# Twelve units of attention loads, each in tiles of its own, and the order of the loads, keys and first weight rounding around them

## The chip, the cores and the metric

The kernel runs on one core of a Trainium2 chip. The metric is the device time of one execution in microseconds (us), lower is better. The core has five engines with an instruction stream each: TensorE (PE, matrix products), VectorE (DVE), ScalarE (ACT), GpSimd (POOL) and SyncE (SP, here only a queue that issues DMA transfers). Each engine takes its instructions strictly in the program's order and waits at the first one whose inputs aren't there.

## What is computed

A decaying linear attention (retention) over 2 batches, 8 heads, 768 positions and 64 channels, and behind it two feed-forward blocks without routing:

```python
for t in range(S):
    state = gamma[None, :, None, None] * state + np.einsum('bhd,bhe->bhde', k[:, :, t], v[:, :, t])
    y[:, :, t] = scale * np.einsum('bhd,bhde->bhe', q[:, :, t], state)
x = y.transpose(0, 2, 1, 3).reshape(B * S, H * D)      # 1536 tokens x 512
x = (x @ w_a) * (x @ w_b) @ w_out                      # hidden 1536
h = x @ w_in; y = np.maximum(0.01 * h, h) @ w_out2     # hidden 2048
```

All arrays are float32.

## The kernel before, in words

**Units.** Attention is cut into twelve units, 3 tiles of 512 tokens times 4 pairs of heads, tile by tile. A unit reads four arrays of 128 x 512 float32 (256 KB each): `qT`, `kT` (turned), `kn` and `vn` (plain); its tiles are called q, k, n and v. The first four units ("wide", u < NPAIR = 4) work in chunks of 128 positions, the other eight in chunks of 64. A unit goes through these steps, each a helper:

- keys (`wide_keys`, L519, `scaled_keys`, L583): kd, the keys n times a decay, on ACT. The wide form reads the constants `table`; the other reads `small`, a part of the tile `second`. Both tables are loaded by DMA (L915, L929)
- queries (`wide_queries`, L525, `scaled_queries`, L588): qs, the queries times a decay, on DVE for u < 2, else on POOL; the second form reads `second`
- scores (L532; L644 for the later units) on PE from k and qs, then P, the masked scores, on DVE (L538; `masked`, L650)
- states (L548; L644) on PE from v and kd, with a chain of small adds on DVE (cb, L552, L556; later units cr, L606, L608). For wide units `wide_spreads` (L562, ACT) copies cb into the tile wk
- within (L570; L644), P times v, and across (L577; L644), qs times the states (wk in the wide units), into one PSUM bank x
- `leave_x`: x is split on ACT and DVE into a rounded part and a remainder (x..h L248, x..l L249), and copied once more for two of the three tiles (xf, L659, L661, ACT). x00 to x03 are the first tile's four pairs, x20 to x23 the second's, x10 to x13 the third's

Every product of the feed-forward blocks is made of three passes of such splits (`mm3`, L254 to L256).

**The loop** runs u from -1 to 11. Turn u makes scores and states of unit u + 1 and within, across and `leave_x` of unit u; keys and queries are made two units ahead: unit 0's before the loop, unit 1's in the turn -1, unit u + 2's late in turn u, for u >= 0. The loads are three units ahead: `loads(u)` issues n, v, q, k of unit u on SP's queue into one of NLOAD = 3 sets of landing tiles, so a load has to wait until the unit three before it has read that set. Units 0 to 2 are loaded ahead of the loop.

**Weights between.** Raw weights (512 KB tiles `raw_a`, `raw_b`, L284) come through the same SP queue, at most NRAW = 4 ahead of the rounding. Each is rounded in three steps on ACT (`begin_weights`, L305, L307, L309) and three on DVE (`round_steps`, L323, L325, L327); then `high(key)` (ACT, L934) and `low()` (DVE, L940) split it into, say, a0h and a0l. `ROUND` says in which turn the steps on DVE run (a0 in 2, b0 in 4, a1 in 5, b1 in 6); `begin_weights` is issued at the end of the turn before, `high` at the end of the same turn, `low` in the next turn.

**Dense work.** `FILL` says how many steps of the first feed-forward products (pa and pb, twelve matmuls of 512 columns for one weight tile, three to a step) PE takes at the end of a turn: 3 in turn 3, 1 in turn 4, then 4 in each turn.

**Slots.** Nearly all big tiles come from one pool of NSLOT = 83 tiles of 256 KB; `slots.done(n)` only counts how many are free for what is planned later.

The order inside a turn of the wide units, before:

```python
if u >= 0:
    loads(u + NLOAD)
leave_x(u)
if u < NPAIR - 1:
    wide_spreads(u + 1)
...
for _ in turn:
    pass
if u >= 0:
    keys(u + 2)
    queries(u + 2)
```

Of the kernel before, what the change touches and what calls it, by code (L numbers as in the profile page):

```python
# [9 lines left out]
F32 = mybir.dt.float32  # L10
# [16 lines left out]
NPAIR = H // 2  # L27
# [8 lines left out]
NRAW = 4  # L36
NEXTRA = 10
NWARM = 10
FILL = {3: 3, 4: 1, 5: 4, 6: 4, 7: 4, 8: 4, 9: 4, 10: 4, 11: 4}
PUMP = {7: 1.2, 8: 1.6, 9: 0.6, 10: 0.6, 11: 0.6}  # L40
ROUND = {2: ("a", 0), 4: ("b", 0), 5: ("a", 1), 6: ("b", 1)}
NBLOCK = 2
NLOAD = 3
CPT = TT // P
COUNT = {"a": FF1, "b": FF1, "wo": FF1, "wi": FF2, "wq": FF2}
HALF = FF2 // 2
# [180 lines left out]
def retention_moe_kernel(ctx: ExitStack, tc: tile.TileContext, ins, out):  # L227
    nc = tc.nc
    qT, kT, kn, vn, wab, wo, w2, head, grow, fine = ins
# [7 lines left out]
    slots = Slots(main, NSLOT)  # L237
# [7 lines left out]
    def split(src, name, new=slots.new):  # L245

        hi, lo = new(F32R, name + "h"), new(F32R, name + "l")
        nc.scalar.copy(hi, src)  # L248
        nc.vector.tensor_sub(lo, src, as32(hi))  # L249
        return hi, lo  # L250
# [24 lines left out]
    source = {"a": (wab, 0), "b": (wab, 1), "wo": (wo, 0), "wi": (w2, 0), "wq": (w2, 1)}  # L275
# [3 lines left out]
    def load_weights():  # L279
        if at["load"] < len(order) and at["load"] < at["round"] + NRAW:  # L280
            kind, f = order[at["load"]]
            src, i = source[kind]
            t = rawp.tile([P, TT], I64, tag="raw", name=f"raw_{kind}{f}")
            nc.sync.dma_start(t, src[f, i])  # L284
            raws[kind, f] = t
            at["load"] += 1
# [7 lines left out]
    def begin_weights():  # L294
        for _ in begin_steps():
            pass
# [16 lines left out]
    def round_steps():  # L313


        n = at["round"]
        key = order[n]
        if key not in begun:
            begin_weights()
        u, sl = begun.pop(key)  # L320
        raws.pop(key)
        ui = u.bitcast(I32)
        nc.vector.tensor_scalar(u, u, TOP, None, op0=ALU.min)  # L323
        yield
        nc.vector.tensor_scalar(ui, ui, 3, None, op0=ALU.logical_shift_left)  # L325
        yield
        nc.vector.tensor_tensor(ui, ui, sl, op=ALU.add)  # L327
        rounded[key] = u
        at["round"] += 1
        load_weights()  # L330
        if key in parked:
            dram[key] = park.tile([P, TT], F32, tag=f"{key[0]}{key[1]}", name=f"{key[0]}{key[1]}")
            nc.gpsimd.dma_start(dram[key], rounded.pop(key))
            slots.done(1)
# [147 lines left out]
    for w in spread:  # L482
        nc.gpsimd.memset(w[0:D, :, 0:D], 0.0)
        nc.gpsimd.memset(w[D:P, :, D:P], 0.0)
    units = [(n, p) for n in range(NTILE) for p in range(NPAIR)]
    landing = {
        name: [slots.new(F32, f"{name}{i}") for i in range(NLOAD)] for name in ("n", "v", "q", "k")
    }
    un = {}
    x, xf = {}, {}  # L490
    heads = [slice(h * D, (h + 1) * D) for h in range(2)]
# [8 lines left out]
    def loads(u):  # L500
        if u >= len(units):
            return
        d = un[u] = {}
        for name, src in (("n", kn), ("v", vn), ("q", qT), ("k", kT)):
            d[name] = landing[name][u % NLOAD]
            nc.sync.dma_start(d[name], src[units[u]])

    flip = heads[::-1]
    cols = [slice(j * P, (j + 1) * P) for j in range(CPT)]
# [17 lines left out]
    @known  # L527
    def wide_scores(u, t, p, d):
        sc = [bank(f"sc{u}{h}") for h in range(2)]
        for c in cols:  # L530
            for h, r in enumerate(flip):
                nc.tensor.matmul(sc[h][:, c], d["k"][r, c], d["qs"][r, c], start=True, stop=True)  # L532
        d["P"] = []
        m = causal.rearrange("p (o t) -> p o t", o=1).to_broadcast([P, CPT, P])
        for h in range(2):
            d["P"].append(slots.new(F32, f"P{u}{h}"))
            n = H + NPAIR + 2 * p + h
            nc.vector.scalar_tensor_tensor(  # L538
                by_chunk(d["P"][h]), by_chunk(sc[h]), wide[:, n:n + 1], m, op0=ALU.mult, op1=ALU.mult
            )  # L540
# [23 lines left out]
    @known  # L564
    def wide_within(u, t, p, d):
        d["x"] = bank(f"x{u}")
        for j, c in enumerate(cols):
            for h, r in enumerate(heads):
                w = d["v"][:, j * P + h * D:j * P + (h + 1) * D]
                nc.tensor.matmul(d["x"][r, c], w, d["P"][h][:, c], start=not j, stop=False)  # L570
# [81 lines left out]
    @known  # L652
    def leave_x(u, n, p, d):
        t = TURN[n]
        x[t, p] = split(d["x"], f"x{t}{p}")
        if t != 1:
            xf[t, p] = slots.new(F32, f"xf{t}{p}")
            if t:
                nc.scalar.mul(xf[t, p], d["x"], -1.0)  # L659
            else:  # L660
                nc.scalar.copy(xf[t, p], d["x"])  # L661
        slots.done(2)
        del un[u]


# [255 lines left out]
    def keep_warm(n):  # L921
        for _ in range(n):
            nc.tensor.matmul(wps, warm[:, 0:P], warm, start=True, stop=True)

    keep_warm(NWARM)
    loads(1)
    loads(2)
    load_weights()
    nc.sync.dma_start(second, fine)  # L929
    lows = []  # L930

    def high(key):
# [4 lines left out]
    def low():  # L937
        while lows:
            key = lows.pop()
            nc.vector.tensor_sub(weights[key][1], rounded.pop(key), as32(weights[key][0]))  # L940
            slots.done(1)
# [16 lines left out]
    def keys(u):  # L958
        (wide_keys if u < NPAIR else scaled_keys)(u)

    def queries(u):
        (wide_queries if u < NPAIR else scaled_queries)(u)

    keys(0)
    queries(0)
    for u in range(-1, len(units)):
        key = ROUND.get(u)
        turn = round_steps() if key else iter(())
        if u < NPAIR:
            if u < NPAIR - 1:  # L970
                wide_scores(u + 1)
            if u < 0:
                keys(1)
                queries(1)
                keep_warm(3)
            if u == 0:
                wide_within(u)
            if u < NPAIR - 1:
                wide_states(u + 1)
            if u < 0:  # L980
                keep_warm(2)
            low()
            if u > 0:
                wide_within(u)
            wide_across(u)
            if u >= 0:
                loads(u + NLOAD)
            leave_x(u)
            if u < NPAIR - 1:
                wide_spreads(u + 1)  # L990
            slots.tick()
            if u == NPAIR - 1:
                issue(states(u + 1))
                issue(scores(u + 1))
                for step in un[u + 1]["adds"]:
                    step()
                masked(u + 1)
            for _ in turn:
                pass
            if u >= 0:  # L1000
                keys(u + 2)
                queries(u + 2)
        else:
            issue(states(u + 1), within(u))
            issue(scores(u + 1), across(u))
            loads(u + NLOAD)
            slots.tick()
            steps = un[u + 1]["adds"] if u + 1 in un else []
            low()
            for step in steps[:3]:  # L1010
                step()
            masked(u + 1)
            for step in steps[3:4]:
                step()
# [3 lines that stand above are left out]
            for step in steps[4:]:  # L1018
                step()
                next(turn, None)  # L1020
            for _ in turn:
                pass
        if u + 1 in ROUND:
            begin_weights()
        if key:
            high(key)
        for _ in range(FILL.get(u, 0)):
            next(dense)
        pump(PUMP.get(u, 0))
        if u in (0, 1, 2, 10, 11):  # L1030
            load_weights()
        if u == 7:
            enqueue_next(2)
            queue.extend(behind)
            behind.clear()
            queue.extend(sub_items(("a", 2), ("b", 2)))
        if u == 8:
            outer = [(xf[d], xf[a]) for d, a in outer]
        if u >= 8:
            for _ in range(2):  # L1040
                d, a = outer.pop(0)
                nc.gpsimd.dma_start(d, a, accum_op=ALU.add)
        if u == 8:
            spare.extend(mixed_items(xf, S, "s", True))
        for _ in range(4 if u > 8 else 0):
            spare.pop(0)[1]()
        slots.tick()
    att.close()
    slots.done(4 * NLOAD)
    extra = ctx.enter_context(tc.tile_pool(name="extra", bufs=1, reuse_waits="tile"))  # L1050

    def tnew(dtype, name):
# [85 lines left out]
    turn = []  # L1138
# [43 lines left out]
    for n in range(NMADE, len(z.plan) - 2):  # L1182
# [12 lines left out]
        name, j = z.plan[n]  # L1195
# [6 lines left out]
        if n in (5 * H1, 6 * H1 + 2):  # L1202
            key = "wi", int(n != 5 * H1)
# [133 lines left out]
    for q in range(HALF):  # L1337
        f = 2 * q
# [52 lines left out]
    for n in range(NMADE2, len(z.plan) - 2):  # L1391
# [14 lines left out]
        name, j = z.plan[n]  # L1406
# [82 lines left out]
```

## Time and profile before

| | us |
|---|---|
| median of 3 runs | 576.54 |
| lowest and highest run | 574.52, 576.55 |
| the profiled execution | 576.74 |
| its span | 575.0 |
| PE busy | 558.7 |
| DVE busy | 457.7 |
| ACT busy | 384.3 |
| POOL busy | 152.9 |

The span runs from the first to the last instruction of one profiled execution; its own time is 1.7 us longer. "Busy" counts compute instructions alone. Matmuls are pipelined, so neighbouring ones overlap in the rows. Idle time of an engine that is not the bound costs nothing. Times in the rows are from the span's start. The granted clock is 1.00 at PE's upper level, 2.4 GHz, and 0.50 at the lower, 1.2 GHz. At the very start the rows read 1.00 too, though ten matmuls of 512 columns take 4.45 us there.

### The profile page before, as it was taken

The numbers are of one execution on the slowest core, as the hardware profiler recorded it, in microseconds if no ns is written. First come the engines' busy times: TensorE is split into PE (matmuls) and PEld (weight loads), VectorE is DVE, ScalarE is ACT, GpSimd is POOL, SyncE is SP. The second block draws the span as 40 slices with busy tenths as digits, with TensorE's granted clock in tenths as the row PEclk, the third lists the DMA queues.
The fourth block names the chain that finished last, engine by engine and source line by source line (L and its number), as shares of the span: only waits on it lengthen the run. The fifth ranks groups of instructions, "written<-read, shape, count | busy, mean of one in ns | idle before, by whom it ended". The sixth has DMA issues, their size and how long they took to land.

```text
span 575.0 us, 10484 instructions
## 1 busy us (share of the span) xinstructions
PE 558.7 (97%) x3751; PEld 469.6 (82%) x3751; DVE 457.7 (80%) x977; ACT 384.3 (67%) x791; POOL 152.9 (27%) x196
## 2 busy tenths in 40 slices
PE   8689899999999999999999999999999999999997
PEld 4667788888888888888888888888888888888886
DVE  3568894878888989679789985898888788999862
ACT  2465746777777987498766755976766986678800
POOL 1112230000323232127660040220333267700000
PEclk9898999999999999999999999999999999999999
DMA  8678762444869898579997163554688699974111
GB/s 314 223 262 293 224 127 83 127 141 142 212 177 254 243 246 253 193 267 270 253 224 195 38 110 92 169 160 126 211 266 249 196 245 239 233 166 142 55 56 55
DMA packets 49764, 108.25 MB, mean 188 GB/s; under 512 B 5936, under 2 KB 13360, under 8 KB 49712
## 3 DMA queue, kind: packets, MB, share of 16 engines
q1 hardware_dynamic: 27504, 66.86, 35.5%
q0 software_dynamic: 21920, 40.38, 33.0%
q8 instruction: 29, 0.48, 0.3%
q10 hardware_dynamic: 288, 0.34, 0.2%
q14 instruction: 23, 0.19, 0.1%
HBM read 74.00 MB, written 18.35 MB: 161 GB/s over the span
## 4 chain that ended last, share of the span: by engine, by line
PE 93%; DVE 3%; ACT 2%; DMA 1%; issue 0%; SPq 0%; DVEq 0%
PE blk L255 12%; PE blk L254 12%; PE blk L256 12%; PE top L255 5%; PE top L254 5%; PE top L256 5%; PE pa L254 4%; PE pb L256 4%; PE pb L254 4%; PE pb L255 4%; PE pa L255 4%; PE pa L256 4%; PE mid L255 3%; PE mid L256 3%; PE mid L254 3%; PE left L255 1%
## 5 line engine op out<-in xcount | busy, mean ns | idle before, releaser
L255 PE MATMUL blk<-form,form 128*128 128x512 f32 (+1 forms) x224 | 75.9, 339 | 0.0
L254 PE MATMUL blk<-form,form 128*128 128x512 f32 (+1 forms) x224 | 75.7, 338 | 0.0
L256 PE MATMUL blk<-form,form 128*128 128x512 f32 (+1 forms) x224 | 75.3, 336 | 0.0
L170 DVE TENSOR_TENSOR form<-g,form 128x512 fp32r<-128x512 f32 x112 | 57.9, 557 | 0.9
L255 PE MATMUL blk<-forma,forma 128*128 128x512 f32 (+1 forms) x168 | 56.9, 339 | 0.0
L254 PE MATMUL blk<-forma,forma 128*128 128x512 f32 (+1 forms) x168 | 56.7, 338 | 0.0
L256 PE MATMUL blk<-forma,forma 128*128 128x512 f32 (+1 forms) x168 | 56.5, 336 | 0.0
L164 ACT CAST form<-g 128x512 fp32r<-128x512 f32 x112 | 52.4, 512 | 4.1 <-DMA g<-g 2.0
L170 DVE TENSOR_TENSOR forma<-h,forma 128x512 fp32r<-128x512 f32 x84 | 43.3, 559 | 4.6 <-ACT forma L164 3.6
L254 PEld LDWEIGHTS blk<-form,form 128*128 128x128 f32 x224 | 42.5, 190 | 5.3
L255 PEld LDWEIGHTS blk<-form,form 128*128 128x128 f32 x224 | 42.5, 190 | 4.7
L256 PEld LDWEIGHTS blk<-form,form 128*128 128x128 f32 x224 | 42.4, 189 | 4.8
L164 ACT CAST forma<-h 128x512 fp32r<-128x512 f32 x84 | 38.9, 511 | 4.8 <-DMA h<-h 4.8
L713 POOL DMA_DIRECT2D farg<-g x26 | 15.6, 615 | 83.2 <-ACT g L1231 61.2
L143 POOL DMA_DIRECT2D h<-h x33 | 33.5, 1181 | 9.5 <-DVE forma L170 5.3
L254 PEld LDWEIGHTS blk<-forma,forma 128*128 128x128 f32 x168 | 31.9, 190 | 3.9
L255 PEld LDWEIGHTS blk<-forma,forma 128*128 128x128 f32 x168 | 31.9, 190 | 3.6
L256 PEld LDWEIGHTS blk<-forma,forma 128*128 128x128 f32 x168 | 31.8, 189 | 3.5
L170 DVE TENSOR_TENSOR form<-wq,form 128x256 fp32r<-128x256 f32 x56 | 23.7, 424 | 10.0 <-ACT form L164 9.8
L713 POOL DMA_DIRECT2D farh<-h x19 | 10.9, 574 | 71.6 <-DVE h L843 49.3
L164 ACT CAST form<-wq 128x256 fp32r<-128x256 f32 x56 | 22.6, 403 | 6.9 <-PE blk L255 2.6
L143 POOL DMA_DIRECT2D g<-farg x22 | 21.9, 1035 | 7.7 <-DVE form L170 3.7
(3066 smaller groups left out, 1694.4 us busy)
## 6 DMA issues: line engine op xcount, KB each, us to landing
raw_wi<-in_w SPq DMA_DIRECT2D x16, 512.0 KB, 4.6
raw_wq<-in_w SPq DMA_DIRECT2D x16, 512.0 KB, 4.8
farg<-g POOLq DMA_DIRECT2D x26, 256.0 KB, 3.7
g<-farg SPq DMA_DIRECT2D x26, 256.0 KB, 7.0
raw_a<-in_wab SPq DMA_DIRECT2D x12, 512.0 KB, 5.0
raw_b<-in_wab SPq DMA_DIRECT2D x12, 512.0 KB, 4.9
raw_wo<-in_wo SPq DMA_DIRECT2D x12, 512.0 KB, 4.5
g<-farg POOLq DMA_DIRECT2D x20, 256.0 KB, 8.1
```

The costliest lines, as they stand in the source:

```text
L143: queue.append((0.0, lambda piece=piece: self.nc.gpsimd.dma_start(self.A(*d[1:], j)[piece], self.A(*x1[1:], j)[piece], accum_op=ALU.add)))
L164: nc.scalar.copy(h, src)
L170: nc.vector.tensor_sub(*todo.pop(0))
L254: nc.tensor.matmul(ps, w[0], x[0], start=first, stop=False, skip_group_check=more)
L255: nc.tensor.matmul(ps, w[0], x[1], start=False, stop=False, skip_group_check=more)
L256: nc.tensor.matmul(ps, w[1], x[0], start=False, stop=last, skip_group_check=more)
L713: nc.gpsimd.dma_start(self.far[t, f], self.tiles[t, f])
```

## The change

- Each unit's q, k, n and v are new tiles of the pool of 83; the landing tiles are gone, and `leave_x` gives back four tiles more per unit.
- The order of a unit's loads is q, k, n, v for the wide units and n, v, q, k for the others.
- Ahead of the loop units 0 to 6 are loaded, with four raw weights and `second` between them: units 0 to 3, raw a0, unit 4, `second`, raw b0, unit 5, raw a1, unit 6, raw b1. In the loop, `loads(u + 8)` stands at the end of turn u. `load_weights` at the end of turns 0 to 2 is gone.
- In the wide turns keys and queries go by `KEYS`: unit 2 in turn -1, unit 3 in turn 0, unit 4 in turn 1, unit 5 in turn 3, so units 2 to 4 are one turn earlier.
- The DVE steps of a0's rounding are spread: two in turn 2, the third in turn 3; `high` of a0 stands at the end of turn 3 in place of turn 2, behind `begin_weights` of b0.
- `FILL` has nothing in turn 3 and four steps in turn 4.

```diff
-FILL = {3: 3, 4: 1, 5: 4, 6: 4, 7: 4, 8: 4, 9: 4, 10: 4, 11: 4}
+FILL = {4: 4, 5: 4, 6: 4, 7: 4, 8: 4, 9: 4, 10: 4, 11: 4}
-NLOAD = 3
+AHEAD = 8
+KEYS = {-1: 2, 0: 3, 1: 4, 3: 5}
...
-    landing = {
-        name: [slots.new(F32, f"{name}{i}") for i in range(NLOAD)] for name in ("n", "v", "q", "k")
-    }
...
         d = un[u] = {}
-        for name, src in (("n", kn), ("v", vn), ("q", qT), ("k", kT)):
-            d[name] = landing[name][u % NLOAD]
-            nc.sync.dma_start(d[name], src[units[u]])
+        source = {"q": qT, "k": kT, "n": kn, "v": vn}
+        for name in "qknv" if u < NPAIR else "nvqk":
+            d[name] = slots.new(F32, f"{name}{u}")
+            nc.sync.dma_start(d[name], source[name][units[u]])
...
-        slots.done(2)
+        slots.done(6)
         del un[u]
...
     keep_warm(NWARM)
-    loads(1)
-    loads(2)
+    for u in range(1, 4):
+        loads(u)
     load_weights()
+    loads(4)
     nc.sync.dma_start(second, fine)
+    load_weights()
+    loads(5)
+    load_weights()
+    loads(6)
+    load_weights()
...
+    turn = iter(())
     for u in range(-1, len(units)):
         key = ROUND.get(u)
-        turn = round_steps() if key else iter(())
+        if u in ROUND:
+            turn = round_steps()
...
-            if u >= 0:
-                loads(u + NLOAD)
             leave_x(u)
...
-            for _ in turn:
-                pass
-            if u >= 0:
-                keys(u + 2)
-                queries(u + 2)
+            next(turn, None)
+            next(turn, None)
+            if u in KEYS:
+                keys(KEYS[u])
+                queries(KEYS[u])
         else:
...
-            loads(u + NLOAD)
...
         if u + 1 in ROUND:
             begin_weights()
-        if key:
+        if u + 1 == NPAIR:
+            key = ROUND[u - 1]
+        if key and u != 2:
             high(key)
         for _ in range(FILL.get(u, 0)):
             next(dense)
         pump(PUMP.get(u, 0))
-        if u in (0, 1, 2, 10, 11):
+        loads(u + AHEAD)
+        if u in (10, 11):
             load_weights()
...
     att.close()
-    slots.done(4 * NLOAD)
```

## Rows read from the trace of the kernel before

**Rows 1.** The page, part 4: shares of the chain that ended last, by engine.

```profile
PE 93%; DVE 3%; ACT 2%; DMA 1%; issue 0%; SPq 0%; DVEq 0%
```

**Rows 2.** Stretches: length, busy (count) of PE, PEld, DVE, ACT, POOL, granted clock, DMA, GB/s.

```profile
3.00:14.00 11.00, 9.60 (x62) 5.20 (x62) 3.77 (x8) 2.51 (x6) 1.27 (x1) 1.00 1.04 384
20.00:24.00 4.00, 4.00 (x48) 3.67 (x46) 1.07 (x4) 0.41 (x1) 0.69 (x1) 0.57 0.47 148
...
60.00:160.00 100.00, 99.76 (x842) 82.78 (x842) 81.08 (x167) 69.53 (x129) 20.18 (x24) 1.00 0.57 149
0.00:60.00 60.00, 47.59 (x834) 36.29 (x835) 34.96 (x85) 29.91 (x56) 11.83 (x16) 0.91 0.81 275
```

**Rows 3.** Waits of PE, 0 to 90: us in total, times, longest.

```profile
PE kv L548 <- ACT kd L519: 4.2, 2, 2.1
PE kv L644 <- issue: 1.7, 1, 1.7
PE x L577 <- ACT wk L562: 1.5, 1, 1.5
PE sc L532 <- DVE qs L525: 1.4, 1, 1.4
...
PE pb L254 <- ACT b1h L934: 1.1, 1, 1.1
PE pb L256 <- DVE b1l L940: 1.1, 1, 1.1
```

**Rows 4.** Timeline of PE: start, us, instruction, count, idle before it.

```profile
1.20 4.45 PE L923 MATMUL warm<-warm 128*128 128x512 bf16 x10 [1.20 <-DVE warm L914]
7.05 2.08 PE L532 MATMUL sc<-qs,k 64*128 64x128 f32 x16 [1.40 <-DVE qs L525]
...
12.48 1.52 PE L532 MATMUL sc<-qs,k 64*128 64x128 f32 x16
...
16.08 1.16 PE L532 MATMUL sc<-qs,k 64*128 64x128 f32 x16
...
33.27 1.25 PE L577 MATMUL x<-qs,wk 128*64 128x128 f32 x12 [1.53 <-ACT wk L562]
...
36.34 0.50 PE L254 MATMUL pa<-x00h,a0h 128*128 128x512 f32 x1
```

**Rows 5.** Timeline of ACT, the same columns.

```profile
4.53 0.91 ACT L519 ACTIVATE kd<-n,table 128x256 f32<-128x256 f32 x2 [1.86 <-DMA table<-in_head]
...
16.20 0.58 ACT L248 CAST x00h<-x 128x512 fp32r<-128x512 f32 x1 [2.95 <-PE x L577]
...
18.14 0.72 ACT L562 COPY wk<-cb 64x192 f32<-64x192 f32 x2
...
26.98 0.65 ACT L305 ACTIVATE a<-raw_a 128x512 f32<-128x512 f32 x1
...
28.17 0.76 ACT L309 ACTIVATE sl<-raw_a 128x512 uint16<-128x512 uint32 x1
...
33.50 0.72 ACT L583 ACTIVATE kd<-n,second 128x512 f32<-128x512 f32 x1
34.12 0.60 ACT L934 CAST a0h<-a 128x512 fp32r<-128x512 f32 x1
...
44.45 0.61 ACT L934 CAST b0h<-b 128x512 fp32r<-128x512 f32 x1
...
50.88 0.60 ACT L934 CAST a1h<-a 128x512 fp32r<-128x512 f32 x1
```

**Rows 6.** Timeline of DVE, the same columns.

```profile
6.29 0.69 DVE L525 TENSOR_TENSOR qs<-q,table 128x512 f32<-128x512 f32 x1 [5.14 <-DMA q<-in_qT]
...
37.87 0.69 DVE L650 TENSOR_TENSOR P<-sc,second 128x512 f32<-128x512 f32 x1
```

**Rows 7.** Timeline of POOL, the same columns.

```profile
12.10 1.27 POOL L525 TENSOR_TENSOR qs<-q,rest 128x512 f32<-128x512 f32 x1 [9.98 <-DMA q<-in_qT]
```

**Rows 8.** Waits of SP's queue, 0 to 60: us in total, times, longest.

```profile
SPq L506 <- PE x L570: 14.7, 3, 5.4
```

## The prediction

> **What bounds the kernel now.** Read the page's chain first: TensorE (PE) carries 93% of the chain that ended last [rows 1]. So the time falls only where PE stands still or runs slowly. The stretches say where: PE is busy for 99.76 of the 100 us from 60 to 160, but for 47.59 of the first 60, at a mean granted clock of 0.91 [rows 2]. Nearly all that PE can gain lies in these 60 us, the attention stage: 12.4 us of standing still and some 5 us of clock. The list of waits names the stops there: 4.2 us in two waits for kd, 1.5 for wk, 1.4 for qs, 1.7 with "issue" (nothing that the profile shows), 1.1 and 1.1 for b1h and b1l [rows 3]. Two stops for kd last 2.1 us each; the four microseconds that follow the first (20 to 24) have PE busy throughout at a granted clock of 0.57, so mostly at the lower level, 1.2 GHz: 4 x 0.43 = 1.7 us lost [rows 2].
>
> **Part by part.** Times are us from the span's start. The sum is made against the profiled execution, 576.74 with a span of 575.0; it is 0.2 above the median of the runs, 576.54.
>
> Start. The warm-up matmuls end at 1.20 + 4.45 = 5.65, the first scores start at 7.05: 1.4 of waiting for qs(0), which starts at 6.29, when q has landed, third in the queue [rows 4, 6]. With q first it lands as n did, no later than the table (4.53, [rows 5]); qs then ends near 5.2, k is second, and scores(0) start at 5.7: 1.35 earlier. From there to scores(1) took 12.48 - 7.05 = 5.4 [rows 4], five more warm-up matmuls among it; they take some 0.44 for 512 columns (4.45 for ten), the pace of the lower clock level. So scores(1) come at 11.1 if the clock does the same again. If it rises sooner because PE no longer stops, VectorE becomes last (P(0) and qs(1) behind scores(0)), some 9.1: estimates from the same rows. I keep 9.1 to 11.1.
>
> Keys a unit earlier. kd(2) and kd(3) are issued one unit sooner on ScalarE (ACT), ahead of x.h, xf and wk, so both waits for kd go: 4.2, and the half-rate stretch behind them. A unit then costs PE what it costs without a wait, 16.08 - 12.48 = 3.60 [rows 4]. Three of them put within(3) at 19.9 to 21.9, done at 21 to 23, against 33.27 for across(3) before.
>
> What is late next: ACT. It is strictly in order, and keys(4) moves ahead of the three begin instructions for a0 and of x(2). keys(4) reads `small`, part of `second`, which now stands in SP's queue behind the 20 tiles of units 0 to 4 and raw a0. Bytes up to it: 20 x 0.262 + 0.524 + 0.266 and 0.338 for table and rest, all by their shapes, = 6.37 MB. While the queue is full the traffic is 384 GB/s (3 to 14, [rows 2]); some 0.2 MB went before 3. The end of a transfer trails this: the 11th tile, q(2), makes 3.22 MB, so 10.8 by that rate, and it landed at 12.1, when GpSimd's qs(2) starts [rows 7]: 1.3 later. So `second` lands at 3 + 6.15/0.384 + 1.3 = 20.3.
>
> The Trainium skill ("DMA: Bandwidth & Descriptors", Specifications) puts the memory limit of one core at about 358 GB/s. By that figure `second` would land near 21.5 and the forecast would be 1.0 us longer, an estimate; the 384 GB/s row disagrees with it, and the row decides.
>
> ACT reaches keys(4) when wk(2) is done, 2.66 after x(1) (x00h at 16.20 to wk's end at 18.14 + 0.72, [rows 5]): 2 x 3.60 + 2.66 after scores(1), 19.0 to 21.0. I take 20.7 for the start of kd(4). Then kd 0.72, begin 1.95 (26.98 to 28.17 + 0.76), x(2)'s leave and wk(3) 2.66 [rows 5]. Begin, leave and wk stand behind kd(4) in ACT's order and PE's across(3) behind them, so across(3) starts at 26.0, 7.3 before 33.27. PE has by then stood for 3 to 5 us, a new and longer stop than the 1.5 for wk that it replaces.
>
> Dense matmuls moved, rounding spread. Before, the first three dense steps (a0 by x00 to x02, from 36.34, [rows 4]) fill PE while VectorE makes P(4), done at 37.87 + 0.69 [rows 6]. Now they come after unit 4, so this cover is gone: x(3) ends at 26.0 + 1.25; P(4) ends 4.06 later (33.27 + 1.25 to 38.56, [rows 4, 6]), at 31.3; scores(4) end 3.1 after across(3) starts (36.34 - 33.27, [rows 4]), at 29.1. PE waits 2.2. The rounding's last step follows P(4) on VectorE, 0.7, to 32.0. ACT meanwhile has x(3) (1.94, 16.20 to 18.14), kd(5) 0.72 and begin b0 1.95, free at 31.9 [rows 5]. So a0h starts at 32.0, only 2.1 before its old 34.12.
>
> But b0h follows sooner. The old a0h stood a unit earlier in the order; now it stands at the end of unit 3, one turn of the loop before b0h. Such a turn (high, low, three adds, P, x low, then xf, begin and the next high on ACT, or the rounding on VectorE) is shown from b0h to a1h: 50.88 - 44.45 = 6.43 [rows 5]. So b0h comes at 38.4, 6.0 before 44.45. In this loop ACT and VectorE are last, not PE: at its end PE stood for b1h and again for b1l [rows 3]. The old 1.7 with "issue" lay in this slack, as b0h came later anyway; its removal earns nothing, and a repeat would mostly cost nothing.
>
> The rest. Turns for a1 and b1 keep 6.43; pb for b1 starts 6.0 earlier. From there PE is the bound (99.76 of 100 us, [rows 2]) and everything moves with it. Loads eight ahead cost SP nothing but queue that it used to hold back (14.7 of its waits were for PE's x, [rows 8]); twelve units, tables and four raws, 15.3 MB, are in by about 44. Raw a2 is issued behind them but is first used after all of attention's roundings. The tiles come from the 83 slots instead of 12 landing tiles; units 0 to 6 take the first 28, so they can't wait for a slot. A later slot wait would hold SP alone: 0 taken, up to 1 kept.
>
> Sum: 7.3 at across(3), 1.3 given back around a0: 576.74 - 6.0 = 570.7.
>
> **The rivals.**
> (A) More gain. `second` and begin don't hold ACT (faster landing, or PE slower to arrive than I think): across(3) at 23, 3.0 better: 567.7. For: 384 GB/s is a mean with the start in it. Against: begin a0 stays ahead of x(2) on ACT whatever lands.
> (B) Most is given back by the clock. The new stops of 3 to 5 and 2.2 us are longer than those after which PE ran at 0.57 [rows 2, 3]; each such stretch costs 1.7 where PE is last. Two of them uncovered, one after across(3) and one at the end of the loop: 574.1; with an uncovered "issue" stop of 1.7, 575.8. I give 574.8. Against: until b1h the loop of ACT and VectorE hides PE's slowness. The Trainium skill ("TensorE: Matmul & The Clock Gate", HAM oscillation) says the same of gaps, that a kernel which stops again and again starts each burst at half rate; by that rule B is the outcome if PE is last in these bursts, and the row at 0.57 agrees that a stop is followed by the lower level.
> (C) Slower. Putting 20 tiles and a raw ahead of `second` delays kd(4), and with it everything on ACT. Each us that `second` lands later than 20.7 is a us lost. At 26.7 the gain is gone; at 29.6 the kernel is slower by 2.9. That needs a rate of 6.15 MB in 25.3 us, 243 GB/s, with a full queue. 275 is the mean of the first 60 us, with the queue often empty, 384 with it full [rows 2]. Time at 29.6: 579.6.
> (D) The change doesn't do what it says, because a unit isn't bound by kd but by its own PE, VectorE and ACT turn; 3.60 per unit in one stretch without a wait speaks against it. About 575.
>
> **How the numbers follow.** Forecast 0.56, A 0.14, B 0.20, C 0.05, D 0.05. Predicted: 570.7. Its own spread is `second` at 20.3 to 21.9, the clock at the start, and slot waits: -1.5 to +2. The range takes in A's upper half and B's lower: 567.5 to 574.5. About 0.5% (2.9 us, below 573.66 or above 579.4) is what can be told from no change. Faster: the forecast, A and some half of B, 0.80; slower: C and a little more, 0.05; the rest 0.15.
>
> **What would show it.** Right: scores(0) at 5.7; no wait for kd at L548; kd(4) at 20 to 21 behind DMA or wk; a wait of across(3) for wk of 3 to 5 us, ending near 26; a wait of PE near 29 to 31 for P(4); b0h near 38.4 and a1h 6.4 behind it; PE without gaps after some 55. Wrong: kd(4) not waiting for anything and across(3) before 24 (A); granted clock 0.5 after 40 with PE back to back (B); `second` after 25 (C); units of 5 us or more between 11 and 22 (D). The prediction is wrong if the first 50 us gain 6 and the rest loses it again.

## The result and the profile after

| us | before | changed |
|---|---|---|
| median (6 runs each) | 575.94 | 569.3 |
| lowest, highest | 572.7, 576.55 | 568.84, 570.68 |
| the profiled execution | 576.74 | 569.38 |
| its span | 575.0 | 567.6 |

The ratio is 0.9899, with a 95% interval of 0.9873 to 0.9926: the kernel is faster, by 6.6 us at the medians and 7.4 from one profiled execution to the other. The forecast was 570.7, from 567.5 to 574.5.

The page, part 4, of the changed kernel: the chain that ended last is still PE's.

```profile
PE 91%; DMA 3%; DVE 3%; ACT 2%; issue 1%; SPq 0%; ACTq 0%
```

The same stretches as in [rows 2], one added (columns as there).

```profile
3.00:14.00 11.00, 10.81 (x142) 7.24 (x142) 6.86 (x16) 3.89 (x9) 1.99 (x2) 1.00 1.05 383
20.00:24.00 4.00, 0.78 (x14) 0.53 (x8) 0.01 (x1) 2.89 (x5) 1.27 (x1) 1.00 1.04 392
27.00:31.00 4.00, 3.75 (x70) 3.25 (x66) 2.04 (x7) 2.43 (x5) 1.27 (x1) 0.67 1.03 388
60.00:160.00 100.00, 99.96 (x730) 83.01 (x729) 81.81 (x165) 70.95 (x132) 17.09 (x22) 1.00 0.56 147
0.00:60.00 60.00, 49.61 (x979) 37.60 (x979) 40.13 (x102) 33.76 (x63) 17.88 (x22) 0.97 0.85 303
```

The first 60 us still hold nearly all that changed: PE is busy 2.0 us longer in them than before, at a mean granted clock of 0.97 in place of 0.91. Behind them PE runs without gaps, as it did. Over the whole span PE stands 2.3 us less (16.3 before, 14.0 now) and is busy 5.1 us less for the same work (558.7, 553.6). Of these 5.1 us, 3.4 are clock: before, three stretches run at about half the clock, and each loses 1.7 us, the one of 20 to 24 [rows 2] and these two; now one does, from 26 to 30.

```profile
27.00:31.00 4.00, 3.93 (x51) 3.87 (x51) 1.07 (x4) 2.02 (x5) 0.00 (x0) 0.58 0.35 135
44.00:48.00 4.00, 4.00 (x101) 3.60 (x91) 2.84 (x7) 2.26 (x4) 1.27 (x1) 0.57 0.94 328
```

The waits of PE (us in total, times, longest) say what is late now:

```profile
PE x L576 <- ACT wk L561: 5.3, 2, 5.1
PE x L643 <- DVE P L649: 1.4, 1, 1.4
PE warm L922 <- DVE warm L913: 1.2, 1, 1.2
PE pb L257 <- DVE b1l L945: 1.1, 1, 1.1
PE pb L255 <- ACT b0h L939: 0.7, 1, 0.7
```

The two waits for kd and the "issue" stop of 1.7 [rows 3] are gone. One long stop, for wk, stands in their place; it ends at 25.86 in the timeline of PE (start, us, instruction, count, idle before it):

```profile
5.58 1.21 PE L531 MATMUL sc<-qs,k 64*128 64x128 f32 x16
...
8.89 1.16 PE L531 MATMUL sc<-qs,k 64*128 64x128 f32 x16 [0.19 <-DVE qs L524]
...
12.13 1.16 PE L531 MATMUL sc<-qs,k 64*128 64x128 f32 x16
...
16.19 1.16 PE L531 MATMUL sc<-qs,k 64*128 64x128 f32 x16
...
25.86 1.92 PE L576 MATMUL x<-qs,wk 128*64 128x128 f32 x12 [5.08 <-ACT wk L561]
...
32.16 0.27 PE L643 MATMUL x<-P,v 64*64 64x64 f32 x2 [1.42 <-DVE P L649]
```

The timeline of ACT shows who held wk: kd(4), which waited for `second`, and begin a0 and x(2) behind it, all ahead of the copy of wk at 25.46. Then it shows the four `high` casts that the prediction went by.

```profile
21.11 0.72 ACT L582 ACTIVATE kd<-n,second 128x512 f32<-128x512 f32 x1 [2.13 <-DMA second<-in_fine]
21.74 0.65 ACT L306 ACTIVATE a<-raw_a 128x512 f32<-128x512 f32 x1
...
25.46 0.72 ACT L561 COPY wk<-cb 64x192 f32<-64x192 f32 x2
...
32.74 0.62 ACT L939 CAST a0h<-a 128x512 fp32r<-128x512 f32 x1 [0.55 <-DVE a L328]
...
39.00 0.60 ACT L939 CAST b0h<-b 128x512 fp32r<-128x512 f32 x1
...
44.85 0.60 ACT L939 CAST a1h<-a 128x512 fp32r<-128x512 f32 x1
...
50.27 0.62 ACT L939 CAST b1h<-b 128x512 fp32r<-128x512 f32 x1 [1.25 <-DVE b L328]
```

In the kernel before b1h stands at 57.29:

```profile
57.29 0.62 ACT L934 CAST b1h<-b 128x512 fp32r<-128x512 f32 x1 [2.22 <-DVE b L327]
```

Against before (across(3) at 33.27, a0h 34.12, b0h 44.45, a1h 50.88 [rows 4, 5], b1h 57.29) they are earlier by 7.4, 1.4, 5.5, 6.0 and 7.0. Far behind, x13h, the last split of attention's results, is 7.2 earlier, and the end of the span 7.4.

### The profile page after: what moved, and what is told of

The parts are those of the page before. It is cut to its first block, busy times and chain, and to the rows that moved or that the text cites. A ratio compares the mean times of both kernels' runs of the same rounds, so it can differ in the third digit from the quotient of the medians.

```text
span 567.6 us, 10485 instructions
## 1 busy us (share of the span) xinstructions
PE 553.6 (98%) x3751; PEld 465.0 (82%) x3751; DVE 456.8 (80%) x977; ACT 384.4 (68%) x791; POOL 153.8 (27%) x196
## 4 chain that ended last, share of the span: by engine, by line
PE 91%; DMA 3%; DVE 3%; ACT 2%; issue 1%; SPq 0%; ACTq 0%
PE blk L256 12%; PE blk L255 12%; PE blk L257 12%; PE top L256 5%; PE top L255 5%; PE top L257 5%; PE pb L257 4%; PE pb L255 4%; PE pb L256 4%; PE pa L255 4%; PE pa L256 4%; PE pa L257 4%; PE mid L256 3%; PE mid L257 3%; PE mid L255 3%; DMA k<-in_kT 2%
```

## The experiments

The theory going in: the earlier keys earn the gain, `second` behind 20 tiles limits it at wk, and between a0h and b1h a loop of VectorE and ACT sets the pace, not PE. The rivals gave the gain to other parts (the start, the free loads), or had it taken by something else (the spread rounding, the clock). Each time is a median beside runs of the kernel before on the same chip, with the ratio and its 95% interval.

**The keys alone**, in the kernel before, with its landing tiles, load order and rounding.

```diff
+KEYS = {-1: 2, 0: 3, 1: 4, 3: 5}
-            if u >= 0:
-                keys(u + 2)
-                queries(u + 2)
+            if u in KEYS:
+                keys(KEYS[u])
+                queries(KEYS[u])
```

> The kernel before with only the order of keys and queries of the changed kernel (unit 2 in turn -1, 3 in turn 0, 4 in turn 1, 5 in turn 3); landing tiles, load order, rounding and dense steps stay. Theory (keys ahead carry the gain, deep loading little): both waits for kd at L548 go; q(3) still lands near 19 to 20 since its landing tile is held, so scores(3) come near 20.7; across(3) starts at 27 to 28 (33.3 before, 25.9 in the changed kernel) and the time is 569.5 to 572. Rival (loads ahead carry it): the waits turn from kd into waits for DMA of the third and fourth unit, across(3) stays later than 31, time 574 or more.

570.9 (0.9923, 0.9896 to 0.995; before 575.56). The keys alone earn 4.7; the whole change earned 6.6 above and 4.5 in a second comparison below, so how much the rest adds to them is not settled by the times. In the trace across(3) starts at 26.12 and b1h at 50.44, 6.9 earlier than before. But x10h, the next split behind b1h, is only 5.3 earlier. Two views show what is late here. Between a1h and b1h, which lie 7.12 apart (5.42 in the changed kernel), VectorE has two passes at over twice their length, and both lie beside GpSimd's qs (43.65 to 44.93 and 47.52 to 48.81):

```profile
43.95 1.53 DVE L941 TENSOR_TENSOR a1l<-a,a1h 128x512 fp32r<-128x512 f32 x1 [1.15 <-ACT a1h L935]
...
47.73 1.35 DVE L324 TENSOR_SCALAR b<-b 128x512 f32<-128x512 f32 x1
```

And behind b1h PE, which has stood for b1h and b1l, is last and at the lower clock level (stretches of one us, columns as in [rows 2]):

```profile
52.00:53.00 1.00, 0.08 (x1) 0.08 (x1) 1.00 (x3) 0.65 (x2) 0.00 (x0) 1.00 0.97 352
53.00:54.00 1.00, 1.00 (x4) 0.76 (x5) 0.93 (x4) 0.00 (x0) 0.10 (x1) 0.69 1.04 291
54.00:55.00 1.00, 1.00 (x4) 0.81 (x3) 1.00 (x4) 0.00 (x0) 1.00 (x1) 0.50 0.37 133
55.00:56.00 1.00, 1.00 (x4) 0.81 (x3) 0.83 (x4) 0.89 (x2) 1.00 (x2) 0.50 0.07 20
56.00:57.00 1.00, 1.00 (x4) 0.37 (x3) 0.00 (x0) 0.32 (x1) 1.00 (x2) 0.60 0.36 63
```

0.31 + 0.50 + 0.50 + 0.40 = 1.7 us of clock are lost there, as much as the 1.6 that the gain shrinks by. This is rival B in small. In the kernel before, the same two stops (1.1 and 1.1, to 59.77) were followed by a clock of 1.00.

**The keys back**, in the changed kernel.

```diff
-KEYS = {-1: 2, 0: 3, 1: 4, 3: 5}
+KEYS = {0: 2, 1: 3, 2: 4, 3: 5}
```

> The changed kernel with keys and queries two units ahead as before (unit 2 in turn 0, 3 in 1, 4 in 2, 5 in 3); all loads stay ahead. Theory: a unit again takes some 7.3 from x to x, through x high, x low, xf, wk, kd, states; PE waits twice about 2 for kd, across(3) starts near 29.5 and the time is 572 to 574, so 3 to 5 of the 6.6 are lost. Rival (loads ahead carry the gain): time within 1 of the changed kernel's 569.3.

571.9 (0.9948, 0.9927 to 0.9968), just under the 572 to 574 that were expected. The two waits for kd are back, across(3) starts at 29.77 and the gain is 3.7.

```profile
PE kv L547 <- ACT kd L518: 4.0, 2, 2.1
```

So the keys are worth 4.7 alone and some 2.6 on top of the rest. With the keys late, kd(4) comes at 30.00 and waits for nothing, and the start's gain comes through in the trace: scores(1) are 3.1 earlier than before (9.37) and across(3) is 3.5 earlier.

**`second` ahead of raw a0 and unit 4**, in the changed kernel.

```diff
+    nc.sync.dma_start(second, fine)
     load_weights()
     loads(4)
-    nc.sync.dma_start(second, fine)
```

> The changed kernel with the table `second` loaded ahead of raw a0 and unit 4 instead of behind them. Theory (kd(4) on ACT waits for `second`, landed at 21.1, and everything behind it on ACT shifts with it): `second` lands near 16, kd(4) starts when wk(2) is done, 19.0, across(3) starts at 23.7, a0h, b0h, a1h, b1h all some 2 earlier, time 567.2 (-2.1). Rival (begin a0 waits for its own raw, or later turns of ACT and VectorE absorb it): across(3) moves by under 1, or moves by 2 and b1h by under 1; time 568.8 to 569.5.

568.04 (0.9879, 0.9855 to 0.9903); its four runs (567.07 to 568.55) lie below the six of the changed kernel. kd(4) starts at 19.15 and waits for nothing, the stop for wk falls from 5.1 to 3.0, across(3) starts 1.9 earlier, and b1h is 2.3 earlier.

```profile
23.94 1.25 PE L576 MATMUL x<-qs,wk 128*64 128x128 f32 x12 [3.04 <-ACT wk L561]
```

The time gains 1.3, less than the 2.1 that was expected: in the profiled execution PE stands 0.7 behind x10h with "issue", which takes the lead from 2.3 there to 1.6 at the end. Rival C's mechanism, `second` late, is thus at work in the changed kernel, only far from the size at which it would have cost the gain.

**The old order of a unit's loads**, in the changed kernel.

```diff
-        for name in "qknv" if u < NPAIR else "nvqk":
+        for name in "nvqk":
```

> The changed kernel with every unit's loads in the old order n, v, q, k. Theory: scores(0) start at 7.05 again, scores(1) near 12.5 instead of 8.9 (1.35 of waiting and a later rise of the clock), but ACT waited 2.1 for `second` in between, so only 3.6 - 2.1 = 1.5 reaches across(3) and the end: time 570.8. Rival 1 (the start passes through whole): +3.6, 572.9. Rival 2 (all of it is hidden behind `second`): 569.3.

569.14 (0.9899, 0.9876 to 0.9922), no different from the changed kernel. The start is late again, by 1.4 and then by 2.5:

```profile
6.97 2.08 PE L531 MATMUL sc<-qs,k 64*128 64x128 f32 x16 [1.32 <-DMA k<-in_kT]
...
11.35 1.16 PE L531 MATMUL sc<-qs,k 64*128 64x128 f32 x16
```

But kd(4) starts at the same 21.11, when `second` lands (GpSimd's qs(4) waits for it to 21.16), and across(3) starts at 25.89 (25.86 in the changed kernel). ACT, busy with wk until 21.01, arrives just then; in the changed kernel it had waited 2.13. The earlier start only makes ACT wait for `second` and PE for wk (5.1 against 3.1), so it earns nothing here. The theory had it earn; the rival, that `second` hides it, was right.

**The rounding of a0 at once**, with the dense steps back in turn 3, in the changed kernel.

```diff
-FILL = {4: 4, 5: 4, ...
+FILL = {3: 3, 4: 1, 5: 4, ...
-            next(turn, None)
-            next(turn, None)
+            for _ in turn:
+                pass
...
-        if u + 1 == NPAIR:
-            key = ROUND[u - 1]
-        if key and u != 2:
+        if key:
             high(key)
```

> The changed kernel with a0's rounding as before (all three steps and the high part at the end of turn 2, dense steps 3 in turn 3 and 1 in turn 4); loads and keys as changed. Theory (the spreading costs: it takes the dense cover from P(4) and puts a0h and a0l into the loop of ACT and VectorE): across(3) stays at 25.9, a0h comes near 26.6, the wait for P(4) goes, b0h comes 11.2 after across(3) as in the kernel before, at 37.1 (39.0 in the changed kernel), time 567.4 (-1.9). Rival (the spreading pays, since the steps of a0 delay x(3)): time 569.3 or more.

570.22 (0.9926, 0.9904 to 0.9948; before 574.2). The theory, which had it gain, fell: a0h comes 5.8 earlier, at 26.91, and nothing comes of it. Behind the stop for wk PE runs at the lower level (0.50 from 25 to 31), so the dense matmuls start 5.2 behind across(3) (3.1 before), the first two of them still slow:

```profile
25.58 1.92 PE L576 MATMUL x<-qs,wk 128*64 128x128 f32 x12 [4.90 <-ACT wk L561]
30.82 0.79 PE L255 MATMUL pa<-x00h,a0h 128*128 128x512 f32 x1
31.41 0.57 PE L256 MATMUL pa<-x00l,a0h 128*128 128x512 f32 x1
```

They stand ahead of unit 4's products on PE and end at 33.59, while P(4) is done at 31.83, so x(4) is late: in ACT's timeline x20h, at 34.18 in the changed kernel, waits 3.0 for PE.

```profile
35.55 0.59 ACT L249 CAST x20h<-x 128x512 fp32r<-128x512 f32 x1 [3.04 <-PE x L643]
```

b0h then comes at 39.98, 1.0 later, and a second half-rate stretch (0.51, 0.50, 0.50 from 42 to 45) follows the wait for it.

**At once, but the dense steps left in turn 4**: as above, without the line of `FILL`.

```diff
-            next(turn, None)
-            next(turn, None)
+            for _ in turn:
+                pass
...
-        if u + 1 == NPAIR:
-            key = ROUND[u - 1]
-        if key and u != 2:
+        if key:
             high(key)
```

> The changed kernel with a0's rounding at once, in turn 2, but the dense steps left in turn 4; it differs from the run with rounding at once only in the three dense steps of turn 3. Theory, new (rounding at once lost because its dense steps fell into the stretch at half rate behind PE's stop of 5 us, which made PE last): with the dense steps in turn 4 unit 4 ends as early as in the changed kernel, b0h comes at 38 to 39, time 568.3 to 569.3. Rival (a0's split on ACT and VectorE ahead of x(3) is what costs): b0h near 40 as with rounding at once, time 570.2.

569.5 (0.9916, 0.9889 to 0.9943; before 574.1), beside 569.62 for the changed kernel. x20h is back at 34.1, b0h comes at 38.02 and b1h at 49.97, 2.0 and 1.3 earlier than with the dense steps in turn 3. So in the trace what hurt was where the dense steps stood; the times, 0.7 apart, do not tell the two apart. The spread of the rounding in itself is worth nothing that can be measured.

**Each scaled qs computed twice on GpSimd**, in the changed kernel; the result is the same.

```diff
-        nc.gpsimd.tensor_mul(by_sub(d["qs"]), by_sub(d["q"]), pair_table(p, 0))
+        for _ in range(2):
+            nc.gpsimd.tensor_mul(by_sub(d["qs"]), by_sub(d["q"]), pair_table(p, 0))
```

> The changed kernel in which GpSimd computes each of the eight later qs twice over, so it is busy next to VectorE for twice as long; nothing else changes. Theory (VectorE's passes stretch while GpSimd computes, and the turn from b0h to a1h is shorter than before, 5.85 for 6.43, because the deep loads let GpSimd finish qs earlier): VectorE operations that overlap one of these take 1.0 to 1.5 in place of 0.42 or 0.69, the turns of 5.8 and 5.4 lengthen to 6.2 to 7, b1h comes 0.6 to 2 later, time 570 to 571.5. Rival (the shorter turns come from the clock or from DMA): VectorE's durations and the time stay, 569.3.

571.71 (0.9951, 0.9934 to 0.9968), some 2 us slower than the changed kernel (569.3, and 569.62 in a second comparison, below), and the fastest of its runs (570.81) is slower than the slowest of both (570.68): b1h is 1.5 later (51.77), and PE stands 1.0 with "issue" behind it. With GpSimd computing almost without a break from 35.46 to 44.34, three of VectorE's passes in this stretch are long:

```profile
37.14 1.32 DVE L326 TENSOR_SCALAR b<-b 128x512 int32<-128x512 int32 x1
38.38 0.27 DVE L608 SCALAR_TENSOR_TENSOR ca<-cr,second,kv 128x64 f32<-128x64 f32 x1
38.57 1.57 DVE L328 CUSTOM_DVE_ANT_0 b<-b,sl 128x1024 uint16<-128x1024 uint16 x1
40.82 1.00 DVE L946 TENSOR_TENSOR b0l<-b,b0h 128x512 fp32r<-128x512 f32 x1 [0.68 <-ACT b0h L940]
```

In the changed kernel they take 0.42, 0.68 and 0.69. The turn from a0h to b0h grows from 6.26 to 7.50, that from b0h to a1h from 5.85 to 6.18. Compute on GpSimd costs VectorE time just where VectorE sets the pace.

**Two or three together.** First `second` early and the rounding at once with the dense steps in turn 3 (the edits above):

> The changed kernel with `second` loaded ahead of raw a0 and unit 4, and a0's rounding and the dense steps as before. Theory (both hold the same chain of ACT and VectorE, one after the other, and PE is not last before b1h): the two gains add, -1.3 and -1.9 from 569.3: 566.1. Rival (PE or VectorE becomes last once one of them is gone): no better than the better of the two alone, 567.4 to 568.

567.89 (0.9901, 0.9873 to 0.993; before 574.2). The two don't add: 566.1 was expected, and nothing that can be measured is gained over the first alone (568.04). Then, on top of it, raw a0 ahead of unit 3 and one step of begin a0 in each gap in which ACT waits for x low (the loads are shown against the changed kernel, and the bookkeeping of begin a0 is left out):

```diff
-    for u in range(1, 4):
-        loads(u)
+    loads(1)
+    loads(2)
     load_weights()
-    loads(4)
+    loads(3)
     nc.sync.dma_start(second, fine)
+    loads(4)
...
+        if u < NPAIR - 1:
+            next(early, None)
...
+    early = begin_steps()
...
```

> As the last, and the three begin instructions of a0 on ACT stand one by one in the three waits of 0.76 in which xf waits for x low (units 0, 1, 2), with raw a0 loaded ahead of unit 3. Theory (ACT's order is what across(3) waits for): ACT loses 1.9 of work between kd(4) and x(2); across(3) comes near 22.2, PE's wait for wk falls to some 1.5, time 564.5. Rival (ACT isn't last any more, or raw a0 ahead of unit 3 delays kd(3) by as much): within 0.7 of the kernel without it.

567.2 (0.9889, 0.9857 to 0.9921). The raw ahead of unit 3 delays n(3), which shows as a wait for DMA in front of kd(3):

```profile
17.00 0.91 ACT L518 ACTIVATE kd<-n,table 128x256 f32<-128x256 f32 x2 [1.31 <-DMA n<-in_kn]
```

So x02h comes at 21.42, as without it (21.44), across(3) at 23.78 (23.76 without it, 22.2 in the theory), and what the gaps give is lost, as the rival had it. Its times spread from 565.75 to 571.24; the profiled one, the slowest, has "issue" stops of 3.0 and 1.8.

**The version that beats both**: the changed kernel with raw a0 behind unit 3, `second` next, and begin a0 in the gaps of units 1 to 3; rounding spread and dense steps in turn 4 as in the changed kernel (the bookkeeping in `begin_steps` is left out below).

```diff
     load_weights()
-    loads(4)
     nc.sync.dma_start(second, fine)
+    loads(4)
...
+        if 0 < u < NPAIR:
+            next(early, None)
...
+    early = begin_steps()
...
-        if u + 1 in ROUND:
+        if u + 1 in ROUND and u != 1:
             begin_weights()
```

> The changed kernel with `second` loaded behind raw a0 and ahead of unit 4, and the three begin instructions of a0 put one by one into ACT's waits of 0.76 for x low in units 1, 2 and 3; the spread rounding and the dense steps in turn 4 stay. Theory (ACT's order sets across(3); the spread keeps the half-rate stretch free of dense work): across(3) at 22.9 against 23.9 with `second` early alone, PE's wait for wk falls from 3.0 to 2, b0h near 35.3, b1h near 47, time some 1 below `second` early alone: 567.0, 2.3 below the changed kernel. Rival (VectorE or PE is last by then): 568 to 569.

566.05 (0.9871, 0.9825 to 0.9917; before 574.1). across(3) starts at 22.89 and b0h at 35.46, as expected; the stop for wk is down to 1.5, and no "issue" stop appears.

```profile
22.89 1.25 PE L576 MATMUL x<-qs,wk 128*64 128x128 f32 x12 [1.52 <-ACT wk L561]
```

The waits of PE, as above:

```profile
PE x L576 <- ACT wk L561: 2.3, 3, 1.5
PE pa L255 <- ACT a1h L941: 1.3, 1, 1.3
```

Beside it, on the same chip, the changed kernel again:

> The changed kernel once more, on the same chip as the two beside it. Every theory: 569.3, within 1, with PE's stops behind matmul 471 and 1232, if there are any, of other lengths than in the first run.

569.62 (0.9924, 0.9895 to 0.9952), so the version is 3.6 faster than the changed kernel at the medians. Beside this set's runs of before (574.1) the changed kernel gains 4.5, in place of the 6.6 above: the kernel before moves by more than the changed one from set to set, and differences of a us between experiments are not told apart. Five of the version's six runs lie between 565.82 and 566.54, one at 570.99, which is what makes its interval wide.

## Why the prediction was right, and where it was off

The profile of before carries the result: PE stood still and ran slowly in the first 60 us only, the keys were late, and once early the next thing late was ACT behind `second`. By its steps:

- **Start.** scores(0) at 5.58 (5.7 forecast), scores(1) at 8.89: the quicker of the two cases. Right as an event, but here it carries no part of the gain: undone, the time is the same, since ACT waits for `second` either way.
- **Keys.** No wait for kd; scores follow each other by 3.24 and 4.06 (3.60 forecast). Right, and the clock goes with it: two of the three half-rate stretches are gone.
- **`second` and ACT.** kd(4) at 21.11 behind DMA (20.7), across(3) at 25.86 (26.0), PE's stop 5.1 (3 to 5). `second` landed 0.8 later than the rows gave (20.3): the term added for the end of a transfer, 1.3, taken at the 11th tile, was too small behind 20 tiles and a raw. The Trainium skill's 358 GB/s ("DMA: Bandwidth & Descriptors", Specifications) gave 21.5 (0.8 behind the 20.7 of the forecast, not the 1.0 that it says), nearer to the 21.1; yet the traffic was 383 GB/s from 3 to 14 and 392 from 20 to 24, so its figure is not what held `second`.
- **Dense moved.** PE waits 1.4 for P(4) (2.2), a0h at 32.74 (32.0). Right in kind (its 4.06 for P(4) is 4.04 by its own rows). The prediction costed the move as cover lost; the runs show that three steps in turn 3 would have been too much cover: behind a half-rate stretch they end 1.8 after P(4) is there, and x(4) comes 1.4 later, where PE without them waits 0.9 for P(4).
- **The turns.** This step failed by size. b0h came at 39.00 (38.4 forecast), then a1h 5.85 behind it and b1h 5.42 behind that, where the prediction kept 6.43 for every turn. It took the turn of before as its plain cost, but that row held VectorE passes stretched by GpSimd. In before's timelines of VectorE and GpSimd:

```profile
44.53 1.27 POOL L588 TENSOR_TENSOR qs<-q,second 128x512 f32<-128x512 f32 x1 [2.79 <-DMA q<-in_qT]
45.09 1.27 DVE L940 TENSOR_TENSOR b0l<-b,b0h 128x512 fp32r<-128x512 f32 x1 [1.13 <-ACT b0h L934]
...
54.90 1.28 POOL L588 TENSOR_TENSOR qs<-q,second 128x512 f32<-128x512 f32 x1 [3.17 <-DMA q<-in_qT]
55.06 1.40 DVE L325 TENSOR_SCALAR b<-b 128x512 int32<-128x512 int32 x1
```

 and in VectorE's timeline of the changed kernel the same two passes:

```profile
39.63 0.69 DVE L945 TENSOR_TENSOR b0l<-b,b0h 128x512 fp32r<-128x512 f32 x1 [1.23 <-ACT b0h L939]
...
49.02 0.42 DVE L326 TENSOR_SCALAR b<-b 128x512 int32<-128x512 int32 x1
```

 0.58 less in one turn and 0.98 in the next: 6.43 - 0.58 = 5.85 as measured, and 57.29 - 50.88 - 0.98 = 5.43 (5.42 measured). In before GpSimd's qs lay beside these passes (44.53 to 45.80, 54.90 to 56.18), having waited 2.8 and 3.2 for the DMA of q, which was held until its landing tile came free. With loads eight ahead q comes sooner, and these two qs (units 7 and 9) start at 32.41 and 37.78. So the loads, which the prediction counted at nothing, are worth some 1.6 us less 0.6 for the late b0h: 7.0 at b1h in place of 6.0. That GpSimd stretches the passes is shown by the run with qs twice. That the free loads are what moves qs away is read from two runs: with the loads ahead and the keys back the turns are 5.87 and 5.36, with the keys alone, on landing tiles, 5.89 and 7.12. The shorter second turn holds in every variant with the loads ahead (5.36 to 5.64). The 0.58 of the first is in part luck: with `second` early alone, a qs still meets a pass there and the turn takes 6.25, in the best version 6.76.
- **PE not last until b1h.** Nearly true in the changed kernel. The half-rate stretch from 26 to 30 (0.67 over 27 to 31) makes across(3) take 1.92; with the old load order, where it takes 1.25 from the same start, a0h comes 0.64 earlier (32.10), but b1h only 0.15 (50.12). False as a rule: the rounding at once made PE last there.
- **The rest moves with it.** 7.0 at b1h, 7.2 at x13h, 7.4 at the end. Right; from 60 to 160 PE stands 0.24 us before [rows 2] and 0.04 in the changed kernel.
- **Rivals.** Of A's larger gain about half came, but not by its mechanism: across(3) was not at 23. B stayed covered here and showed in two of the experiments, the keys alone and the rounding at once with the dense steps in turn 3; the rule of the Trainium skill that the prediction set beside B ("TensorE: Matmul & The Clock Gate", HAM oscillation) agrees with both of them, but not with every stop: before, the two stops for b1h and b1l left the clock at 1.00. C was small. D fell with the pace of the units.

## What to carry to other kernels

When a wait is removed, follow the in-order engine behind it to the next transfer or table that it will ask for, and move that too: a table of 0.27 MB in the queue and three ACT steps behind it were worth 3.6 us more. A duration read from one stage holds what ran beside it there, so compare the same pass in two places (0.42 and 1.40 us) before it is used as a plain cost. An earlier start earns nothing while a later join waits for something else, and work moved forward can land in a stretch where the clock is low.

## What the runs showed of the hardware

- **VectorE beside GpSimd.** A pass of 128x512 that starts while GpSimd's multiply runs takes up to 1.72 in place of 0.69 when it reads two SBUF tiles (a0l, b0l, a1l), and up to 1.50 in place of 0.42 in the rounding's passes with one input. Its length depends on when it starts, its end does not: in the first 62 us of all runs here such a pass ends some 0.55 (two tiles) or 0.28 (one input) after the multiply does, so it waits for the multiply rather than running slowly. Before, b0l ends at 46.36 behind a qs that ends at 45.80. The other way round GpSimd waits; in the changed kernel the pass keeps its 0.68 and the qs takes 1.76 in place of 1.27:

```profile
37.72 0.68 DVE L328 CUSTOM_DVE_ANT_0 b<-b,sl 128x1024 uint16<-128x1024 uint16 x1
37.78 1.76 POOL L587 TENSOR_TENSOR qs<-q,second 128x512 f32<-128x512 f32 x1 [1.40 <-DVE b L326]
```

 Not all wait: in the changed kernel P at 35.14 and x20l at 35.88, each with one input in PSUM (the banks of the matrix products), take 0.68 beside a qs from 35.09 to 36.38. The Trainium skill says this ("GPSIMD Engine Reference", Specifications): the SBUF interface is shared with VectorE, in contention with its two-port modes and with instructions of two SBUF inputs. The rows with two SBUF inputs agree; in which mode the passes with one input run, no row shows.
- **"issue" stops of PE.** Wherever one stands, in before and in all variants, it is behind 471, 597, 1105 or 1232 matmuls of the program (1233 in one run), so 126, 508 and 127 apart, and its length differs from run to run: 1.73 behind 471 in before, 0.15 behind 597 in the changed kernel and none when that was run again, 3.00 behind 471 and 1.83 behind 1232 in the one with raw a0 ahead of unit 3, none in the best version. The spacings are near multiples of 127 matmuls, each with its weight load; no run here shows the cause.
- **The clock after a stop.** After PE's stop of 5.1 us the granted clock was 0.60 in the first us and 0.50 in the next two. After 1.5 us in before (31.74 to 33.27) it stayed at 1.00. In the best version it stayed at 1.00 after one stop of 1.5 (to 22.89) and fell to 0.50 behind two shorter ones (0.74 and 0.94, to 28.05). With `second` early alone it stayed at 1.00 for five us after a stop of 3.0 (to 23.94) and fell only near 30. What decides between these isn't settled here.
